# Strassen products and output units of a second feed-forward layer: the order in which they are issued

## The chip, the cores and the metric

One core of a Trainium2 chip runs the whole program. The metric is the device time of one execution in microseconds; the kernel before takes 963.16 us in the median of three runs (962.7 to 963.23).

## The reference

Linear attention over 4 batches of 8 heads (576 positions, 64 dimensions, 128 random features in two signs), and behind it two feed-forward layers on the 2304 tokens of 512 channels. Only the second layer bears on the change:

```python
def _moe2_ref(x, w_in, w_out):
    h = x @ w_in              # 2304x512 by 512x2048
    r = np.maximum(h, 0.0)
    g = r * r
    return (g @ w_out).astype(np.float32)   # 2304x2048 by 2048x512
```

## The kernel before, in words

Every fp32 matrix product is made of three matmuls on fp32r values: an operand is split into a high part (a rounded copy, ScalarE) and a low part (the difference, VectorE), and high x high, high x low and low x high are added up in PSUM.

The program has three stages: attention, the first layer (`feed_forward`, blocks of 512 tokens: `G1`, the elementwise part, `G2`), and the second layer. Within a stage the order is written out by hand: each engine runs its instructions in the order of the program text, and waits by semaphores where data or a buffer isn't ready.

The second layer works on 3 groups of 768 tokens. For a group, 8 *pairs* of 128-column chunks of the hidden dimension are computed, so 24 pairs s = 0 to 23 in all. The four quarters 11, 12, 21 and 22 of a pair's hidden block (two chunks by two halves of 384 tokens) come from **seven products** in Strassen's way instead of eight (`product`, L598, its matmuls at L611). A product is 6 matmuls of 128x128 weights by 384 columns. The products write two PSUM banks in turn: 0, 2, 4, 6 the one and 1, 3, 5 the other; with the next pair the two change places. Between the products `quarters` (L616) takes the partial sums out and combines them:

- after product 0, 2 and 4 ScalarE copies the bank (s1, s2, s3: L628, L637, L642); products 2, 4 and 6 add to that bank, so they must wait for these copies;
- after product 1 VectorE adds s1 and the other bank to quarter 11 (L634), after product 3 it makes a part of 12 (L640), which L644 lessens by s3, and after product 5 it makes 21 (L647);
- after product 6 VectorE finishes 12 (L652) and ScalarE makes 22 by a Relu (L655), then a square (L656).

`square` (L625, VectorE) applies relu and square to 11, 21 and 12. `hi_lo` (L590) splits a finished quarter: high part at L592 on ScalarE, low part at L593 on VectorE.

The **output units** (`unit`, L658, matmuls at L666) multiply the quarters of the pair before by the output weights: 12 units for each pair, unit n of three matmuls of 512 columns, that adds into one of six other PSUM banks. Units 0 to 5 use quarters 11 and 21 in turn, units 6 to 11 use 12 and 22. In the last pair of a group every second unit is followed by the eviction of its bank (L676 on ScalarE or L678 on VectorE) and a store.

`second_step(s, k)` (L701) issues product k of pair s, its `quarters`, `UNITS_AT[k]` units of pair s - 1, the pieces of operand preparation that fall there (`refill`, L682: subtractions L445 and splits L451 and L452 at pairs 7, 8, 15 and 16), and the DMA that reads back a piece of weights for pair s + 2 (`read_back`, L695, issued on SP at L493). `second_layer` (L715) calls it for s = 1 to 24 and k = 0 to 6, and after each step `convert_late`. Pair 0's products are issued earlier, among the last `G2` of the first layer (`FIRST_AT`, L728), followed by the evictions of the first layer's last block (L402, L404).

`convert_late(now)` (L577) issues what is due before `now + 1` of the preparation of 16 tiles of output weights, which come in 64-bit form. A tile with the time `at` of `LATE_AT` is loaded by SP (L472) at `at - 2`; at `at` its *words* are taken apart (L238, L240, both ScalarE); at `at + 2` they are *joined* (L259, L261, L268 on VectorE, then L263 on POOL); at `at + 4` the tile is *split* (L281 on ScalarE, L285 on VectorE). The clock of these times counts 7 for a pair:

```python
LATE_AT = (-1, 1, 3, *range(5, 44, 3))
LATE_STAGE = 2

def convert_late(now):
    while late_events and late_events[0][0] < now + 1:
        late_events.pop(0)[1]()
```

So tiles 3 to 15 have the times 5, 8, 11, ... 41, and the last split is due at 45, in pair 6.

Of the kernel before, what the change touches and what calls it, by code (L numbers as in the profile page):

```python
# [12 lines left out]
ACTF = mybir.ActivationFunctionType  # L13
# [13 lines left out]
    ("A11", "B11", 0, True), ("A12", "B21", 1, True), ("S2", "T2", 0, False), ("S4", "B22", 1, True),  # L27
    ("S3", "T3", 0, False), ("A22", "T4", 1, True), ("S1", "T1", 0, False),
)
UNITS_AT = (2, 2, 2, 2, 2, 1, 1)  # L30
AHEAD_TILES = tuple(("in", n) for n in range(16))
AHEAD_FIRST, AHEAD_NEXT, AHEAD_STAGE, AHEAD_LOAD = 14.0, 8.6, 7.0, 9.5
LATE_AT = (-1, 1, 3, *range(5, 44, 3))
# [130 lines left out]
def attention_ffn_kernel(  # L164
# [11 lines left out]
    nc = tc.nc  # L176
# [12 lines left out]
    def f(t):  # L189
        return t.bitcast(F32)  # L190

    with tc.manual_schedule():
# [15 lines left out]
        def bank(tag, shape=(P, 512), name=None):  # L208
            return ps.tile(list(shape), F32, tag=tag, name=name or tag, bufs=BUFS[tag])
# [225 lines left out]
        NG, NP = NT // GROUP, KFF // 2  # L435
        raw_x, wc, spill, h2_t, g2_t, b2 = {}, {}, {}, {}, {}, {}
# [140 lines left out]
# [3 lines that stand above are left out]
# [10 lines left out]
        def hi_lo(s, name):  # L590
            g, t = quarter(s, name), h2_t.pop((s, name))
            nc.scalar.activation(out=g[:, 0], in_=t, func=ACTF.Copy)  # L592
            nc.vector.tensor_tensor(out=g[:, 1], in0=t, in1=f(g[:, 0]), op=ALU.subtract)  # L593
# [4 lines left out]
        def product(s, k):  # L598
            if k == 0 and s == 0:
                b2["m"] = [bank("pj", name="m") for _ in range(2)]  # L600
            p = s % NP
            wn, xn, to, start = PRODUCTS[k]
            i = next(i for i in range(4) if wn in PIECES[i])
            o = 2 * P * PIECES[i].index(wn)
            wh, wl = (w_piece(s, i, hl)[:, o:o + 2 * P] for hl in range(2))
            xh, xl = x_parts(xn)
            m = banks(s)[to]
            for q in range(2):
                sl = slice(q * P, (q + 1) * P)
                for n, (l, r) in enumerate(((wh, xh), (wh, xl), (wl, xh))):  # L610
                    nc.tensor.matmul(  # L611
                        out=m, lhsT=l[:, sl], rhs=r[:, q], start=start and q == 0 and n == 0, stop=q == 1 and n == 2,
                        skip_group_check=True,
                    )

        def quarters(s, k):  # L616

            a, b = banks(s)

            def new(name, tag="pq"):  # L620
                t = h2_t[s, name] = work(tag, [P, HALF], F32, "t")
                return t

            def square(t):
                nc.vector.scalar_tensor_tensor(out=t, in0=t, scalar=0.0, in1=t, op0=ALU.max, op1=ALU.mult)  # L625

            if k == 0:
                nc.scalar.activation(out=new("s1", "kq"), in_=a, func=ACTF.Copy)  # L628
                if s > 0:
                    hi_lo(s - 1, "12")  # L630
                    hi_lo(s - 1, "22")
            elif k == 1:
                t = new("11")
                nc.vector.tensor_tensor(out=t, in0=b, in1=h2_t.pop((s, "s1")), op=ALU.add)  # L634
                square(t)
            elif k == 2:
                nc.scalar.activation(out=new("s2", "kq"), in_=a, func=ACTF.Copy)  # L637
                hi_lo(s, "11")
            elif k == 3:
                nc.vector.tensor_tensor(out=new("12"), in0=b, in1=h2_t.pop((s, "s2")), op=ALU.add)  # L640
            elif k == 4:
                nc.scalar.activation(out=new("s3", "pk"), in_=a, func=ACTF.Copy)  # L642
                t = h2_t[s, "12"]
                nc.vector.tensor_tensor(out=t, in0=t, in1=h2_t[s, "s3"], op=ALU.subtract)  # L644
            elif k == 5:
                t = new("21")
                nc.vector.tensor_tensor(out=t, in0=h2_t.pop((s, "s3")), in1=b, op=ALU.subtract)  # L647
                square(t)
            else:
                hi_lo(s, "21")  # L650
                t = h2_t[s, "12"]
                nc.vector.tensor_tensor(out=t, in0=a, in1=t, op=ALU.add)  # L652
                square(t)
                t = new("22")
                nc.scalar.activation(out=t, in_=a, func=ACTF.Relu)  # L655
                nc.scalar.activation(out=t, in_=t, func=ACTF.Square)  # L656

        def unit(s, n):  # L658
            m, f_ = divmod(n, 2)
# [39 lines left out]
                    read_piece(s + 2, i)  # L699

        def second_step(s, k):  # L701
            if s < NG * NP:
                product(s, k)
                quarters(s, k)
            elif k == 0:
                for name in ("12", "22"):
                    hi_lo(s - 1, name)
            if s > 0:
                n0 = sum(UNITS_AT[:k])
                for n in range(n0, n0 + UNITS_AT[k]):  # L710
                    unit(s - 1, n)
            refill(s, k)
            read_back(s, k)

        def second_layer():  # L715
            for s in range(1, NG * NP + 1):
                for k in range(7):
                    second_step(s, k)
                    convert_late(7 * s + k)

        def share(j, i):
            if j == 0 and i >= START_0:
# [67 lines left out]
        with ExitStack() as actx:  # L790
# [172 lines left out]
            run, steps = {}, {}  # L963
# [164 lines left out]
```

## Time and profile before

| | |
|---|---|
| Median of three runs | 963.16 us (962.7 to 963.23) |
| The profiled execution's own time | 963.75 us |
| Its span, first to last instruction | 962.0 us |
| TensorE busy | 953.5 us (99%) |
| VectorE busy | 657.4 us (68%) |
| ScalarE busy | 536.9 us (56%) |
| GpSimd busy | 169.0 us (18%) |
| TensorE's granted clock over the span | 0.999 of full speed |
| Second layer: from pair 0's first product to the last matmul | 574.6 to 957.9 us |

The span is the profiled execution's; what lies between it and the execution's time is outside of the trace. In the trace PE is TensorE, PEld its weight loads, DVE VectorE, ACT ScalarE, POOL GpSimd, SP the engine that issues nearly all DMAs (SPq its queue). A matmul's end is modelled, so the distance of starts is the measure of TensorE's rhythm. In the timeline neighbours of one line are merged (x6 is six instructions), and brackets give the engine's idle time before an instruction and what ended it.

### The profile page before, as it was taken

Reading aid. Unit: us, or ns where it says so; the run is one execution under the profiler, and the core shown is the slowest. Engines: PE = TensorE matmul, PEld = TensorE weight load, DVE = VectorE, ACT = ScalarE, POOL = GpSimd, SP = SyncE. Lnnn points to the kernel's source line nnn. Section 1 sums busy time; section 2 is a strip of 40 time slices with the busy share of each in tenths; the row PEclk is TensorE's granted clock in tenths of the full one; section 3 lists DMA queues with packets and bytes.
Section 4 is the critical chain, followed back from the end, with each engine's and each line's share of the span. In section 5 each row is a group of like instructions: output and inputs, shape, how many; then the busy total and the mean of one; then the engine's idle time right before and its main releaser. Section 6 shows DMA issues by size and latency. Waiting matters only on the chain.

```text
span 962.0 us, 15555 instructions
## 1 busy us (share of the span) xinstructions
PE 953.5 (99%) x5865; PEld 824.9 (86%) x5865; DVE 657.4 (68%) x1137; ACT 536.9 (56%) x1053; POOL 169.0 (18%) x146
## 2 busy tenths in 40 slices
PE   8999999999999999999999999999999999999998
PEld 7878888788899888888888888989889898989897
DVE  6787887589967777867867667777663444744344
ACT  4988886667766656666655654555352323423223
POOL 1666765100002033213200011221000000000000
PEclk9999999999999999999999999999999999999999
DMA  7566633152021155334335206656563435544411
GB/s 245 174 204 229 189 121 101 32 204 79 1 89 41 29 190 168 120 131 155 132 132 149 71 22 208 199 184 190 172 194 112 121 113 184 164 138 126 118 36 65
DMA packets 52282, 128.26 MB, mean 133 GB/s; under 512 B 6384, under 2 KB 12144, under 8 KB 52208
## 3 DMA queue, kind: packets, MB, share of 16 engines
q1 hardware_dynamic: 52064, 127.21, 41.2%
q8 instruction: 46, 0.75, 0.3%
q14 instruction: 28, 0.23, 0.1%
q10 hardware_dynamic: 144, 0.07, 0.0%
HBM read 102.99 MB, written 24.19 MB: 132 GB/s over the span
## 4 chain that ended last, share of the span: by engine, by line
PE 94%; DMA 2%; ACT 2%; DVE 1%; POOL 0%; SPq 0%; issue 0%; DVEq 0%; ACTq 0%; POOLq 0%
PE acc L385 21%; PE acc L666 20%; PE m L611 18%; PE h L314 7%; PE h L315 7%; PE h L316 7%; PE kv L867 5%; PE nm L913 3%; PE pj L833 2%; PE nm L921 2%; PE tp L890 1%; PE kv L875 1%; PE pj L842 1%; DMA raw<-in_dram 1%; ACT eq L901 1%; ACT e L859 0%
## 5 line engine op out<-in xcount | busy, mean ns | idle before, releaser
L666 PE MATMUL acc<-w,g 128*128 128x512 f32 x864 | 226.0, 394 | 0.0
L385 PE MATMUL acc<-g,w 128*128 128x512 f32 (+1 forms) x960 | 208.6, 368 | 0.0
L385 PEld LDWEIGHTS acc<-g,w 128*128 128x128 f32 x960 | 168.0, 189 | 30.5 <-DVE g L345 0.6
L666 PEld LDWEIGHTS acc<-w,g 128*128 128x128 f32 x864 | 159.7, 188 | 23.3
L611 PE MATMUL m<-xc,wc 128*128 128x384 f32 x864 | 173.7, 336 | 0.8 <-DVE t L634 0.8
L611 PEld LDWEIGHTS m<-xc,wc 128*128 128x128 f32 x864 | 154.5, 188 | 14.2 <-DVE t L634 1.3
L314 PE MATMUL h<-xs,w 128*128 128x512 f32 (+1 forms) x320 | 117.9, 369 | 0.0
L315 PE MATMUL h<-xs,w 128*128 128x512 f32 (+1 forms) x320 | 117.7, 368 | 0.0
L316 PE MATMUL h<-xs,w 128*128 128x512 f32 (+1 forms) x320 | 117.7, 368 | 0.0
L593 DVE TENSOR_TENSOR g<-t,g 128x384 fp32r<-128x384 f32 x96 | 53.6, 579 | 77.5 <-ACT g L592 77.4
L342 ACT ACTIVATE g<-tr 128x512 fp32r<-128x512 f32 (+1 forms) x80 | 47.0, 589 | 69.2 <-PE acc L385 46.7
L263 POOL TENSOR_TENSOR mag<-mag,raw 128x512 int32<-128x512 int32 x36 | 48.1, 1337 | 213.1 <-ACT tr L335 92.1
L592 ACT ACTIVATE g<-t 128x384 fp32r<-128x384 f32 x96 | 47.3, 518 | 64.8 <-DVE t L625 64.5
L337 DVE SCALAR_TENSOR_TENSOR tr<-tr,h 128x512 f32<-128x512 f32 (+1 forms) x80 | 50.5, 631 | 35.5 <-ACT tr L335 35.2
L345 DVE TENSOR_TENSOR g<-tr,g 128x512 fp32r<-128x512 f32 (+1 forms) x80 | 52.8, 660 | 24.7 <-ACT g L342 24.7
L314 PEld LDWEIGHTS h<-xs,w 128*128 128x128 f32 x320 | 60.3, 189 | 10.2 <-issue 0.2
L316 PEld LDWEIGHTS h<-xs,w 128*128 128x128 f32 x320 | 60.3, 188 | 10.1
L315 PEld LDWEIGHTS h<-xs,w 128*128 128x128 f32 x320 | 60.4, 189 | 9.9
L848 DVE TENSOR_REDUCE m<-pj 128x4 f32<-128x512 f32 (+1 forms) x80 | 49.9, 624 | 19.3 <-PE pj L833 11.7
L867 PEld LDWEIGHTS kv<-v,e 128*128 128x128 f32 x512 | 60.1, 192 | 3.4 <-issue 1.8
L867 PE MATMUL kv<-v,e 128*128 128x65 f32 x512 | 62.1, 274 | 0.7 <-ACT e L859 0.6
L330 DVE SCALAR_TENSOR_TENSOR tr<-tr,h 128x512 f32<-128x512 int32 (+1 forms) x80 | 50.2, 628 | 16.0 <-ACT tr L328 15.5
(92 smaller groups left out, 1339.8 us busy)
## 6 DMA issues: line engine op xcount, KB each, us to landing
wc<-sp SPq DMA_DIRECT2D x72, 512.0 KB
raw<-in_dram SPq DMA_DIRECT2D x48, 512.0 KB
xbuf<-in_dram SPq DMA_DIRECT2D x16, 512.0 KB
sp<-xbuf SPq DMA_DIRECT2D x15, 512.0 KB
kq<-in_dram SPq DMA_DIRECT2D x16, 384.0 KB
wc<-sp SPq DMA_DIRECT2D x24, 256.0 KB
v<-in_dram SPq DMA_DIRECT2D x16, 330.0 KB
dn<-db SPq DMA_DIRECT2D x32, 144.0 KB
```

What stands on the lines that cost most here:

```text
L314: nc.tensor.matmul(out=hps, lhsT=ih[:, kk, :], rhs=xh, start=kk == 0, stop=False)
L315: nc.tensor.matmul(out=hps, lhsT=ih[:, kk, :], rhs=xl, start=False, stop=False)
L316: nc.tensor.matmul(out=hps, lhsT=il[:, kk, :], rhs=xh, start=False, stop=kk == KDM - 1)
L330: nc.vector.scalar_tensor_tensor(out=r, in0=t.bitcast(I32), scalar=-C1, in1=h_t[c], op0=ALU.mult, op1=ALU.add)
L337: nc.vector.scalar_tensor_tensor(out=t, in0=r, scalar=1.0, in1=h_t.pop(c), op0=ALU.subtract, op1=ALU.mult, reverse0=True)
L345: nc.vector.tensor_tensor(out=g[:, 1], in0=t, in1=f(g[:, 0]), op=ALU.subtract)
L385: nc.tensor.matmul(out=acc[m][:, 0:n], lhsT=l, rhs=r, start=c == 0 and i == 0, stop=c == KFF - 1 and i == 2)
L593: nc.vector.tensor_tensor(out=g[:, 1], in0=t, in1=f(g[:, 0]), op=ALU.subtract)
L611: nc.tensor.matmul(out=m, lhsT=l[:, sl], rhs=r[:, q], start=start and q == 0 and n == 0, stop=q == 1 and n == 2, skip_group_check=True,)
L666: nc.tensor.matmul(out=acc[m], lhsT=g[:, l, sl], rhs=w[:, r], start=p == 0 and f_ == 0 and i == 0, stop=p == NP - 1 and f_ == 1 and i == 2,)
L848: nc.vector.tensor_reduce(out=m[:, 0:n], in_=pj[:, 0:n, :], axis=AX.X, op=ALU.max, apply_absolute_value=True)
L867: nc.tensor.matmul(out=acc[:, s, h, 0:D + 1], lhsT=e[:, t, s, :], rhs=v_t[u][:, t, h, 0:D + 1], start=t == 0 and h == 0 and s == 0, stop=F ...
```

## The change

The table `UNITS_AT` (2, 2, 2, 2, 2, 1, 1 units behind the seven products) goes. In its place a pair's products are issued in three runs, products 0 and 1, products 2 and 3, and products 4, 5 and 6, with four units of the pair before behind each run. `convert_late` is called after each unit instead of after each step, with a `now` that grows by 7/12 from unit to unit, starting from 7s.

The square of 11 moves from behind product 1 to behind product 2, and its split from product 2 to product 3. The squares of 21, 12 and 22 and the splits of 21, 12 and 22 are put into a list `owed` when product 6 is issued, and one entry is taken from it after each unit: four behind the last run of the pair, two behind the first two units of the next. Before pair 1 two entries are taken at once. In the last step, that has units alone, `refill` and `read_back` are no longer called.

```diff
--- before.py
+++ after.py
@@ -27,7 +27,7 @@
     ("A11", "B11", 0, True), ("A12", "B21", 1, True), ("S2", "T2", 0, False), ("S4", "B22", 1, True),
     ("S3", "T3", 0, False), ("A22", "T4", 1, True), ("S1", "T1", 0, False),
 )
-UNITS_AT = (2, 2, 2, 2, 2, 1, 1)
+SHORT_RUNS = (((0, 1), 4), ((2, 3), 4), ((4, 5, 6), 4))
 AHEAD_TILES = tuple(("in", n) for n in range(16))
 AHEAD_FIRST, AHEAD_NEXT, AHEAD_STAGE, AHEAD_LOAD = 14.0, 8.6, 7.0, 9.5
 LATE_AT = (-1, 1, 3, *range(5, 44, 3))
@@ -613,6 +613,8 @@
                         skip_group_check=True,
                     )
 
+        owed = []
+
         def quarters(s, k):
 
             a, b = banks(s)
@@ -626,18 +628,15 @@
 
             if k == 0:
                 nc.scalar.activation(out=new("s1", "kq"), in_=a, func=ACTF.Copy)
-                if s > 0:
-                    hi_lo(s - 1, "12")
-                    hi_lo(s - 1, "22")
             elif k == 1:
                 t = new("11")
                 nc.vector.tensor_tensor(out=t, in0=b, in1=h2_t.pop((s, "s1")), op=ALU.add)
-                square(t)
             elif k == 2:
                 nc.scalar.activation(out=new("s2", "kq"), in_=a, func=ACTF.Copy)
-                hi_lo(s, "11")
+                square(h2_t[s, "11"])
             elif k == 3:
                 nc.vector.tensor_tensor(out=new("12"), in0=b, in1=h2_t.pop((s, "s2")), op=ALU.add)
+                hi_lo(s, "11")
             elif k == 4:
                 nc.scalar.activation(out=new("s3", "pk"), in_=a, func=ACTF.Copy)
                 t = h2_t[s, "12"]
@@ -645,15 +644,16 @@
             elif k == 5:
                 t = new("21")
                 nc.vector.tensor_tensor(out=t, in0=h2_t.pop((s, "s3")), in1=b, op=ALU.subtract)
-                square(t)
             else:
-                hi_lo(s, "21")
                 t = h2_t[s, "12"]
                 nc.vector.tensor_tensor(out=t, in0=a, in1=t, op=ALU.add)
-                square(t)
                 t = new("22")
                 nc.scalar.activation(out=t, in_=a, func=ACTF.Relu)
-                nc.scalar.activation(out=t, in_=t, func=ACTF.Square)
+                owed.extend((
+                    lambda: square(h2_t[s, "21"]), lambda: hi_lo(s, "21"), lambda: square(h2_t[s, "12"]),
+                    lambda: nc.scalar.activation(out=t, in_=t, func=ACTF.Square),
+                    lambda: hi_lo(s, "12"), lambda: hi_lo(s, "22"),
+                ))
 
         def unit(s, n):
             m, f_ = divmod(n, 2)
@@ -699,24 +699,28 @@
                     read_piece(s + 2, i)
 
         def second_step(s, k):
-            if s < NG * NP:
-                product(s, k)
-                quarters(s, k)
-            elif k == 0:
-                for name in ("12", "22"):
-                    hi_lo(s - 1, name)
-            if s > 0:
-                n0 = sum(UNITS_AT[:k])
-                for n in range(n0, n0 + UNITS_AT[k]):
-                    unit(s - 1, n)
+            product(s, k)
+            quarters(s, k)
             refill(s, k)
             read_back(s, k)
 
         def second_layer():
-            for s in range(1, NG * NP + 1):
-                for k in range(7):
-                    second_step(s, k)
-                    convert_late(7 * s + k)
+            steps = NG * NP
+            for _ in range(2):
+                owed.pop(0)()
+            for s in range(1, steps + 1):
+                n, now = 0, 7.0 * s
+                for ks, units in SHORT_RUNS:
+                    if s < steps:
+                        for k in ks:
+                            second_step(s, k)
+                    for _ in range(units):
+                        unit(s - 1, n)
+                        n += 1
+                        if owed:
+                            owed.pop(0)()
+                        convert_late(now)
+                        now += 7 / 12
 
         def share(j, i):
             if j == 0 and i >= START_0:
```

## Rows read from the trace of the kernel before

**Rows 1.** The page, engines and groups (busy us, mean ns, idle us)
```profile
PE 953.5 (99%) x5865; PEld 824.9 (86%) x5865; DVE 657.4 (68%) x1137; ACT 536.9 (56%) x1053; POOL 169.0 (18%) x146
...
L611 PE MATMUL m<-xc,wc 128*128 128x384 f32 x864 | 173.7, 336 | 0.8 <-DVE t L634 0.8
...
L593 DVE TENSOR_TENSOR g<-t,g 128x384 fp32r<-128x384 f32 x96 | 53.6, 579 | 77.5 <-ACT g L592 77.4
```

**Rows 2.** Timeline, product 0 of pairs 4 and 5 (start us, us, engine, line)
```profile
635.85 1.22 PE L611 MATMUL m<-xb,wc 128*128 128x384 f32 x6
...
651.54 1.22 PE L611 MATMUL m<-xb,wc 128*128 128x384 f32 x6
```

**Rows 3.** Timeline from pair 1's product 0 to pair 2's
```profile
587.47 1.20 PE L611 MATMUL m<-xb,wc 128*128 128x384 f32 x6
...
589.48 0.49 ACT L655 ACTIVATE t<-m 128x384 f32<-128x384 f32 x1 [1.09 <-DVE t L652]
...
589.96 1.28 DVE L404 COPY ot<-acc 128x512 f32<-128x512 f32 x2
...
590.03 1.31 PE L611 MATMUL m<-xc,wc 128*128 128x384 f32 x6
...
604.48 1.22 PE L611 MATMUL m<-xb,wc 128*128 128x384 f32 x6
```

**Rows 4.** Timeline, pair 0's products among the first layer's last matmuls
```profile
574.59 1.23 PE L611 MATMUL m<-xb,wc 128*128 128x384 f32 x6
...
576.69 2.92 PE L385 MATMUL acc<-g,w 128*128 128x512 f32 x12
...
579.45 3.31 PE L611 MATMUL m<-xc,wc 128*128 128x384 f32 x18
...
580.72 0.49 ACT L637 ACTIVATE t<-m 128x384 f32<-128x384 f32 x1 [3.36 <-PE m L611]
...
582.60 2.92 PE L385 MATMUL acc<-g,w 128*128 128x512 f32 x12
```

**Rows 5.** Timeline, pair 7 from product 4 to its Relu
```profile
692.66 1.21 PE L611 MATMUL m<-xc,wc 128*128 128x384 f32 x6
...
693.90 0.49 ACT L642 ACTIVATE t<-m 128x384 f32<-128x384 f32 x1 [3.23 <-PE m L611]
...
697.03 0.55 DVE L647 TENSOR_TENSOR t<-t,m 128x384 f32<-128x384 f32 x1
...
698.09 0.95 DVE L452 TENSOR_TENSOR xc<-xr,xc 128x768 fp32r<-128x768 f32 x1
...
700.07 0.49 ACT L655 ACTIVATE t<-m 128x384 f32<-128x384 f32 x1 [1.34 <-DVE t L652]
```

**Rows 6.** Timeline, pair 4, a join's first instruction and the splits behind it
```profile
646.52 0.42 DVE L259 TENSOR_SCALAR mag<-mag 128x512 f32<-128x512 f32 x1
...
649.79 0.63 ACT L281 ACTIVATE w<-mag 128x512 fp32r<-128x512 f32 x1 [1.34 <-POOL mag L263]
...
650.46 0.69 DVE L285 TENSOR_TENSOR w<-mag,w 128x512 fp32r<-128x512 f32 x1
```

**Rows 7.** Timeline, pair 3, product 3, a load and its words
```profile
627.48 1.21 PE L611 MATMUL m<-xc,wc 128*128 128x384 f32 x6
...
629.46 0.33 SPq L472 DMA_DIRECT2D raw<-in_dram  x1
...
634.03 0.67 ACT L238 ACTIVATE mag<-raw 128x512 f32<-128x512 f32 x1 [2.39 <-DMA raw<-in_dram]
```

**Rows 8.** Two stretches at the end: busy us by engine, clock, DMA
```profile
957.00:958.00 1.00, 0.93 (x5) 0.42 (x3) 1.00 (x2) 0.00 (x0) 0.00 (x0) 1.00 0.90 336
...
960.00:962.00 2.00, 0.00 (x0) 0.00 (x0) 0.00 (x0) 0.00 (x0) 0.00 (x0) 0.54 0.21 77
```

**Rows 9.** Timeline, TensorE's first two groups of matmuls
```profile
1.58 2.50 PE L820 MATMUL nm<-eq 128*128 128x512 f32 x5 [1.58 <-DVE eq L814]
...
4.01 3.79 PE L833 MATMUL pj<-wph,kq 64*128 64x128 f32 x32
```

## The prediction

> **What bounds the kernel now.** I read the page first: TensorE is busy 953.5 us of a span of 962.0, and at the products it idles 0.8 us in all, behind VectorE's L634 [rows 1]. So TensorE's own rhythm and its stalls set the time; another engine counts only where it makes TensorE wait. Then I read the timeline of the second layer step by step. A step, from one pair's product 0 to the next pair's, takes 635.85 to 651.54 = 15.69 us for pair 4 [rows 2], and the other 21 of pairs 2 to 23 are like it. Pair 1's is longer, 587.47 to 604.48 = 17.01 us [rows 3]: there the 0.8 us lies. So two things can be won in the second layer: the cost of switching between products and units, and the 1.3 us of pair 1. Whatever else the change moves can only make a new wait.
>
> **Longer runs.** The trace has runs of the new lengths, where pair 0's products lie among the first layer's last matmuls, which have the shape of a unit's. Twelve matmuls of products take 574.59 to 576.69 = 2.10 us, twelve of unit shape 2.76, eighteen of products 579.45 to 582.60 = 3.15 [rows 4]. The new step is 2 x 2.10 + 3.15 + 3 x 2.76 = 15.63 against 15.69. Rounding leaves 0.04 to 0.06; I take 0.05 x 22 = **-1.1 us**.
>
> **Which distance shrinks.** A product's sum is read by ScalarE or VectorE before the product after next may write that bank. The reader starts 1.24 us after the product's first matmul (692.66 to 693.90) and takes 0.49 [rows 5]. Nearly all these distances are now two products and four units, 4.9 us, and were no longer before. One shrinks: from product 4 to product 6, by way of ScalarE's copy s3 (L642). Before, three units and product 5 lay between; now product 5 alone does, so product 6 is due 2.10 us after product 4's start, and the copy ends at 1.73 if ScalarE is free. The pattern stands in the trace once: products 2, 3 and 4 of pair 0 are one run, the copy L637 ends at 580.72 + 0.49 = 581.21, product 4 is due at 579.45 + 2.10 = 581.55, and the run shows no wait [rows 4]. A free ScalarE thus costs nothing; one that is late by more than 0.34 us stalls TensorE. What stands ahead of s3 in ScalarE's queue decides.
>
> **What is put ahead of it.** The late weights are converted by due times: words (ScalarE), join (VectorE, then POOL), split (ScalarE's high half waits for POOL). What is due at 7s + 5 was issued after step 5, so behind s3; now it is issued behind the eighth unit, just ahead of product 4 and s3. By LATE_AT that is a split in pairs 1 and 4, words in pair 3, a join (no ScalarE) in 2 and 5, nothing from 6 on.
>
> *Pair 4.* The join is due behind the fifth unit, after product 3's L640 and the low half of 11. Counting from the start of product 3's last matmul: L640 0.37 to 0.92, the low half (0.58 [rows 1]) to 1.5, the join from 1.55, and ScalarE's split 3.27 later (646.52 to 649.79 [rows 6]), 4.82. s3 starts 0.55 behind it and ends at 5.86. Product 6 was due at 0.17 + 2.76 + 1.07 + 1.04 = 5.04. From a release to the matmul it is 0.06 (L655 ends 589.97, the matmul starts 590.03), and a run that begins from a stall takes 0.1 more [rows 3]: **+1.0 us**. Before, this very split waited 1.34 us for POOL [rows 6] with nothing urgent behind it. Behind s3 stand VectorE's L644 and L647 and the Relu; four units come before those are wanted, so the stall is paid once.
>
> *Pair 3.* Its words wait for a load that SP can issue only behind the read-back that waits for product 3. Product 3's last matmul started at 627.48 + 0.87 = 628.35, the load was issued at 629.46, and the words began at 634.03, after ScalarE had waited 2.39 us for the DMA [rows 7]: 5.68 behind that last matmul. Two words and then s3, each about 0.58 behind the one before, put s3's end at 7.3 against 5.04: **+2.4 us**. The wait was there before; what covered it was s3's place ahead of it, and that is gone.
>
> *Pair 1.* VectorE enters it with the first layer's last evictions (1.28 us [rows 3]), and the squares and splits that now stand behind the units queue behind those. From product 6 of pair 0 (586.43) on: L652 587.67 to 588.2, evictions to 589.5, square 21 to 590.1, ScalarE's high half to 590.65, low half to 591.25, L634 591.85, square 12 592.4, a low half of weights (0.69 [rows 6]) 593.15, join. Its split starts 3.27 later, 596.45, and ends at 597.1 [rows 6]; low half of weights 597.8, low half of 22 598.35, square 11 598.95, L640 599.5, low half of 11 600.1, next join; its split at 603.4, s3 to 604.45. Product 6 starts at 604.5, the next pair at 604.5 + 1.07 + 0.1 + 2.76 = 608.4 against 604.48 [rows 3]: **+3.9 us**, the old wait included. TensorE's earlier stalls in this step hide behind the chain.
>
> *Pairs 7 and 15* fill the next group's operands. Behind product 4 VectorE has L644, two fill steps, L647 (697.03), the low half L452 (698.09, so 5.43 after product 4's start, 0.95 long), then L652 (0.55), and 0.1 later ScalarE's Relu L655, which waits for L652 [rows 5]. The Relu ends 7.55 after product 4's start; the next pair's product 1 is due at 2.10 + 1.04 + 2.76 + 1.07 = 6.97. With release and restart 0.7 each: **+1.4 us**. Before, six units lay in that distance; now four.
>
> **The clock.** In pair 1 TensorE would idle from 601.1 to 604.5. At the trace's end it falls idle near 957.9, and the granted clock of 960 to 962 averages 0.54 [rows 8], so it went to 1.2 GHz after some 2.2 us without a matmul. What a fall costs is bounded by the start of the trace: five matmuls of 512 columns take 2.50 us, twice the later rate, and 32 small ones until 7.80 are slow too [rows 9]; 6.2 us at half rate lose 3.1. Between 0 and 3.1 I take the middle, **+1.5 us**, once, as only pair 1's gap is clearly longer than that of the end. The Trainium skill (TensorE: Matmul & The Clock Gate, "HAM oscillation — how this bites in real kernels") warns that idle gaps between bursts of matmuls let the clock be gated down again. The end of this trace agrees; by that rule alone, with a fall in pair 1 and one in pair 3, the term would be twice as large.
>
> **Elsewhere nothing.** The moved squares and splits add no instruction; in a usual step 21 is wanted by the next step's second unit, over 4 us later, and 12 and 22 by its seventh and eighth. SP's and POOL's queues keep their order. The last step loses its idle fill steps, for which nobody waits.
>
> **The sum:** -1.1 + 1.0 + 2.4 + 3.9 + 1.4 + 1.5 = +9.1 us. On the profiled execution's own 963.75 (span 962.0) that is 972.9; the median of the runs, 963.16, lies 0.6 lower, so I predict 972.3.
>
> **The rivals.** *The clock stays up*: the same waits without the fall, 970.8. For it: the only fall shown is at the end. Against it: the gap of 3.4 us. Chance 0.25. *A late copy in every step*: something small sits on ScalarE, and s3 misses its 0.34 us by 0.15 in 23 steps, +3.5: 975.8. Against it: ScalarE idles 3.23 us before s3 [rows 5]. Chance 0.08. *Faster*: ScalarE and VectorE run the conversions during the four units and s3 is never late; then 1.1 and 1.3 are won, 960.8. It decides at product 6: s3 done before 2.0 us after product 4's start, in every pair. For it: the clean run of eighteen [rows 4]. Against it: ScalarE's waits of 1.34 and 2.39 us in the very instructions that now precede s3 [rows 6, 7]. Chance 0.07. *About the same*: one conversion alone stalls, and the gains pay for it, 962 to 965. Chance 0.05. The forecast has 0.55.
>
> **How the numbers follow.** A measurement of this kernel tells about 0.2%, 1.9 us, from no change. Forecast, steady clock and late copies lie above that: slower 0.88, same 0.05, faster 0.07. The range goes down to 967.5 (no fall, pair 1 at 1.5, pair 3 at 1.5) and up to 976.5, where a fall at 3.1, a second one, or the late copies lie. It leaves out the faster and the unchanged case and the tails.
>
> **What would show it.** The waits of the changed kernel should name TensorE at L611 behind ScalarE's L642 in pairs 1, 3 and 4 alone, some 3.4, 2.3 and 0.9 us, and behind L655 as pairs 8 and 16 begin, with L281 or L238 right ahead of each late L642. A usual step should take 15.64, and the granted clock should dip once, behind 601. I am wrong if TensorE's idle time in the second layer is under 1.3 us, or if L642 is late in steps without a conversion.

## The result and the profile after

| | before | after |
|---|---|---|
| Median (four runs each) | 962.93 us (962.12 to 963.23) | 971.73 us (971.1 to 972.27) |
| Profiled execution | 963.75 us | 972.19 us |
| Its span | 962.0 us | 970.4 us |
| Granted clock over the span | 0.999 | 0.996 |

The fourth run of the kernel before (962.12 us) moves its median from the 963.16 that the prediction started from to 962.93. The ratio is 1.0091, with a 95% interval of 1.0076 to 1.0106: the kernel became slower by 0.9%.

In the listing after the change the copies s1, s2 and s3 stand at L630, L635 and L641, the additions to 11, 12 and 21 at L633, L638 and L646, L649 ends quarter 12, L651 is the Relu and L627 the square. L611 and L666 are the products' and the units' matmuls as before. First the products' group on the page of the changed kernel (columns as in [rows 1]):

```profile
L611 PE MATMUL m<-xc,wc 128*128 128x384 f32 x864 | 164.2, 337 | 5.9 <-ACT t L641 5.1
```

The products' group was idle for 0.8 us behind VectorE [rows 1]; it is idle for 5.9 now, and 5.1 of it stands behind ScalarE's copy s3. The waits of the changed kernel over the second layer (us in total, times, longest) say how often:

```profile
PE m L611 <- ACT t L641: 5.1, 3, 2.9
...
PE m L611 <- ACT t L651: 0.6, 2, 0.3
```

So there are three waits for s3 and two for the Relu. The timeline gives each its place. In it are product 0 of pairs 1 to 6 and what stood ahead of each late copy and ahead of the late Relu of pair 7:

```profile
586.75 1.21 PE L611 MATMUL m<-xb,wc 128*128 128x384 f32 x6
...
602.13 0.63 ACT L281 ACTIVATE w<-mag 128x512 fp32r<-128x512 f32 x1 [1.66 <-POOL mag L263]
602.67 0.47 ACT L641 ACTIVATE t<-m 128x384 f32<-128x384 f32 x1
...
603.20 1.32 PE L611 MATMUL m<-xc,wc 128*128 128x384 f32 x6 [2.88 <-ACT t L641]
604.36 4.50 PE L666 MATMUL acc<-w,g 128*128 128x512 f32 x12
604.56 0.56 DVE L649 TENSOR_TENSOR t<-m,t 128x384 f32<-128x384 f32 x1
605.03 0.55 DVE L627 SCALAR_TENSOR_TENSOR t<-t 128x384 f32<-128x384 f32 x1
...
608.70 1.23 PE L611 MATMUL m<-xb,wc 128*128 128x384 f32 x6
...
624.34 1.23 PE L611 MATMUL m<-xb,wc 128*128 128x384 f32 x6
...
632.25 0.33 SPq L472 DMA_DIRECT2D raw<-in_dram  x1
...
636.58 0.66 ACT L238 ACTIVATE mag<-raw 128x512 f32<-128x512 f32 x1 [4.54 <-DMA raw<-in_dram]
637.68 0.47 ACT L641 ACTIVATE t<-m 128x384 f32<-128x384 f32 x1
...
638.20 1.81 PE L611 MATMUL m<-xc,wc 128*128 128x384 f32 x6 [1.86 <-ACT t L641]
...
643.69 1.23 PE L611 MATMUL m<-xb,wc 128*128 128x384 f32 x6
...
655.04 0.63 ACT L281 ACTIVATE w<-mag 128x512 fp32r<-128x512 f32 x1 [2.97 <-POOL mag L263]
655.57 0.47 ACT L641 ACTIVATE t<-m 128x384 f32<-128x384 f32 x1
...
656.10 1.32 PE L611 MATMUL m<-xc,wc 128*128 128x384 f32 x6 [0.41 <-ACT t L641]
...
660.02 1.23 PE L611 MATMUL m<-xb,wc 128*128 128x384 f32 x6
...
675.66 1.23 PE L611 MATMUL m<-xb,wc 128*128 128x384 f32 x6
...
706.42 0.96 DVE L452 TENSOR_TENSOR xc<-xr,xc 128x768 fp32r<-128x768 f32 x1 [0.45 <-ACT xc L451]
...
707.94 0.49 ACT L651 ACTIVATE t<-m 128x384 f32<-128x384 f32 x1 [1.55 <-DVE t L649]
...
708.48 1.31 PE L611 MATMUL m<-xc,wc 128*128 128x384 f32 x6 [0.32 <-ACT t L651]
```

In pair 1 the split L281 waits for POOL, s3 waits behind the split, and product 6 behind s3. In pair 3 the words L238 wait for their load, in pair 4 a split waits for POOL again. In pair 7 the Relu is started only after L649, which stands behind the low half L452 on VectorE. The twelve matmuls behind product 6 of pair 1 are recorded with 4.50 us, where the same run took 2.92 among pair 0's products [rows 4]. The windows of the changed kernel (columns as in [rows 8]) say why:

```profile
604.70:608.00 3.30, 3.30 (x10) 2.56 (x9) 2.64 (x6) 2.49 (x5) 0.00 (x0) 0.50 0.50 159
...
638.20:638.70 0.50, 0.50 (x3) 0.50 (x4) 0.50 (x2) 0.00 (x0) 0.00 (x0) 1.00 0.56 213
...
638.80:642.10 3.30, 3.30 (x11) 2.84 (x10) 1.86 (x4) 1.40 (x4) 0.00 (x0) 0.50 0.29 68
```

The granted clock is 0.50, so 1.2 GHz, behind both gaps, and 1.00 before the second fall. The step lengths, as distances from one product 0 to the next in the two timelines, are the account of the change:

| step (pair) | before | after | difference |
|---|---|---|---|
| 1 | 17.01 | 21.95 | +4.94 |
| 3 | 15.69 | 19.35 | +3.66 |
| 4 | 15.69 | 16.33 | +0.65 |
| 8 and 16 | 15.69 each | 16.23 each | +1.08 |
| the other 17 of pairs 2 to 22 | 15.687 each | 15.640 each | -0.80 |
| all | | | **+9.53** |

The span grew by 8.4 (970.4 - 962.0). Of the rest -0.72 lies ahead of pair 0's first product (573.87 against 574.59, [rows 4]); in the ten experiments, which also keep that part's work, it lies between 572.8 and 574.4, so I take it for scatter between executions. Another -0.4 lies behind pair 23's product 0: 28.06 us from there to the end of the span before, 27.69 after. Most of it, 0.3, lies behind the last matmul (4.03 us against 3.73, and 3.7 in every experiment too). In the kernel before the copy of the last bank but one (L678, 957.49) stands on VectorE behind two splits of the last step's idle fill steps (L452, 955.55, 2.02 us together); in the changed kernel the same copy waits for TensorE alone. That these fill steps delayed the last stores is likely, but no run takes them out alone.

### The profile page after: what moved, and what is told of

It reads as the page before. It is cut to its first block, busy times and chain, and to the rows that moved or that the text cites. A ratio compares the mean times of both kernels' runs of the same rounds, so it can differ in the third digit from the quotient of the medians.

```text
span 970.4 us, 15613 instructions
## 1 busy us (share of the span) xinstructions
PE 957.7 (99%) x5865; PEld 827.4 (85%) x5865; DVE 643.5 (66%) x1133; ACT 532.4 (55%) x1050; POOL 169.1 (17%) x146
## 4 chain that ended last, share of the span: by engine, by line
PE 89%; DVE 3%; ACT 3%; DMA 3%; POOL 1%; issue 0%; SPq 0%; ACTq 0%; POOLq 0%; DVEq 0%
PE acc L666 19%; PE acc L385 18%; PE m L611 17%; PE h L314 6%; PE h L315 6%; PE h L316 6%; PE kv L871 6%; PE nm L917 3%; PE pj L837 3%; PE nm L925 2%; DMA raw<-in_dram 2%; PE tp L894 1%; DMA sp<-xbuf 1%; PE kv L879 1%; PE pj L846 1%
## 5 line engine op out<-in xcount | busy, mean ns | idle before, releaser
L666 PE MATMUL acc<-w,g 128*128 128x512 f32 x864 | 213.4, 396 | 0.4 <-DVE g L593 0.2
L666 PEld LDWEIGHTS acc<-w,g 128*128 128x128 f32 x864 | 163.1, 190 | 33.3 <-DVE g L593 1.4
L611 PE MATMUL m<-xc,wc 128*128 128x384 f32 x864 | 164.2, 337 | 5.9 <-ACT t L641 5.1
L611 PEld LDWEIGHTS m<-xc,wc 128*128 128x128 f32 x864 | 152.9, 188 | 11.6 <-ACT t L641 6.1
L593 DVE TENSOR_TENSOR g<-t,g 128x384 fp32r<-128x384 f32 x96 | 51.3, 552 | 16.1 <-ACT g L592 16.0
L334 ACT ACTIVATE tr<-tr 128x512 f32<-128x512 f32 (+1 forms) x80 | 46.5, 581 | 21.5 <-DVE tr L332 21.1
```

The lines of the kernel that those rows point to most:

```text
L611: nc.tensor.matmul(out=m, lhsT=l[:, sl], rhs=r[:, q], start=start and q == 0 and n == 0, stop=q == 1 and n == 2, skip_group_check=True,)
L666: nc.tensor.matmul(out=acc[m], lhsT=g[:, l, sl], rhs=w[:, r], start=p == 0 and f_ == 0 and i == 0, stop=p == NP - 1 and f_ == 1 and i == 2,)
```

## The experiments

All start from the changed kernel. A time without an interval is that of one execution; beside it stands the kernel before on the same chip (one execution too, or the median of 21). The two bounds behind a ratio are its 95% interval. Steps are read from the timelines as above. The theory on trial: the loss is made of separate late entries in ScalarE's queue, one behind each late conversion and one behind the fill steps, and of clock falls that follow the longest gaps. The rival: the new order as such (longer runs, less distance, splits moved behind units) costs.

**One load a unit earlier (pair 3 alone).**

```diff
-                events += stages(("out", n), LATE_AT[n], LATE_STAGE, LATE_STAGE, load, split)
+                events += stages(("out", n), LATE_AT[n], LATE_STAGE, LATE_STAGE + (n == 10), load, split)
```

> Only tile 10's load of late weights is moved, one unit of the due times earlier, so that SP issues it ahead of product 3 of pair 3 instead of behind it. Theory (in pair 3 product 6 waits for s3, s3 for the words ahead of it on ScalarE, and those for this load): the words begin before product 4 ends, product 6 of pair 3 follows product 5 after 1.04 us, TensorE's idle 1.86 us there goes and with it the second fall of the clock; step 3 takes 15.64 instead of 19.35, the total falls by 3.7 to about 968. Pairs 1 and 4 stay as they are (21.95 and 16.33). Rival (the two words themselves, or the fuller VectorE, make s3 late, not the load): step 3 stays above 16.5 and the total within 1 us of 971.7.

It took 967.57 us (before: 963.89). Step 3 fell from 19.35 to 15.64; steps 4, 8 and 16 stayed, step 1 was 22.13. Its timeline in pair 3:

```profile
626.17 0.36 SPq L472 DMA_DIRECT2D raw<-in_dram  x1
...
631.05 0.66 ACT L238 ACTIVATE mag<-raw 128x512 f32<-128x512 f32 x1
...
633.17 3.31 PE L611 MATMUL m<-xc,wc 128*128 128x384 f32 x18
634.43 0.49 ACT L641 ACTIVATE t<-m 128x384 f32<-128x384 f32 x1 [2.15 <-PE m L611]
```

Issued one unit earlier in the program, the load no longer stands behind the read-back that waits for product 3. The words are done before product 4 begins, products 4 to 6 run as eighteen matmuls without a break, and s3 waits for TensorE, not the reverse. The whole of step 3's loss, the clock fall included, hung on one place in SP's queue.

**Two splits a unit later (pairs 1 and 4).** The splits of tiles 4 and 11 alone come one unit later, so behind s3.

```diff
-                yield at + 2 * d, lambda: sends.append(split(t, at))
-                yield at + 2.5 * d, lambda: sends.pop(0)()
+                late = 0.5 if t[1] in (4, 11) else 0.0
+                yield at + (2 + late) * d, lambda: sends.append(split(t, at))
+                yield at + (2.5 + late) * d, lambda: sends.pop(0)()
```

> Only the splits of late tiles 4 and 11 come one unit of the due times later, so that they stand behind product 6 instead of right ahead of s3. Theory (s3 waits behind a split that waits for POOL): in pair 4 the stall goes, step 4 takes 15.64 instead of 16.33. In pair 1 s3 then waits only for the words of tile 5, which ended at 600.5, so product 6 starts near 601 instead of 603.2, the gap is under 1 us, the clock does not fall there, and step 1 takes about 18.2 instead of 21.95. Pair 3 stays at 19.35. Total about 967.3. Rival (VectorE's backlog in pair 1 holds s3 by way of the high half of 11, whatever the split does): step 1 stays above 21.

It took 967.74 us (before: 963.89). Step 4 fell to 15.62, step 1 to 18.30; step 3 stayed at 19.40. Its timeline in pairs 1, 3 and 4 (lines one higher than in the changed kernel), and the window behind pair 3's product 6:

```profile
600.97 1.33 PE L612 MATMUL m<-xc,wc 128*128 128x384 f32 x6 [0.59 <-ACT t L642]
...
634.45 1.48 PE L612 MATMUL m<-xc,wc 128*128 128x384 f32 x6 [1.90 <-ACT t L642]
...
649.65 3.31 PE L612 MATMUL m<-xc,wc 128*128 128x384 f32 x18
```

```profile
635.50:638.00 2.50, 2.50 (x8) 2.02 (x7) 1.44 (x3) 1.38 (x4) 0.00 (x0) 0.50 0.38 80
```

Pair 4's wait was the split alone: its products 4 to 6 are eighteen matmuls without a break. In pair 1 a gap of 0.59 us is left, for s3 there now stands behind the words of tile 5. Pair 3 is as it was, with its fall.

**The fill steps one product earlier (pairs 8 and 16).**

```diff
-                todo = ((), (0,), (3, 4), (1,), (2, 5), (6,), ())[k]
+                todo = ((), (0,), (3, 4), (1, 2, 5), (6,), (), ())[k]
```

> Only the order of the next group's operand preparation in pairs 7 and 15 changes: steps 2 and 5 are issued behind product 3 instead of product 4, step 6 behind product 4 instead of 5. Theory (product 1 of the next pair waits for the Relu, the Relu for L649 behind these on VectorE): steps 8 and 16 take 15.64 instead of 16.23, the total falls by 1.2 to about 970.5. Rival (four units are too short a distance for the Relu in any order): steps 8 and 16 stay at 16.2. A third outcome, a new stall in steps 7 and 15 because L640 or s3 is now late: these steps rise above 15.64.

It took 969.17 us (before: 963.89). Steps 8 and 16 went from 16.23 to 15.64. Its timeline in pair 3 and at the end of pair 7:

```profile
637.92 1.32 PE L611 MATMUL m<-xc,wc 128*128 128x384 f32 x6 [1.99 <-ACT t L641]
...
702.58 0.55 DVE L646 TENSOR_TENSOR t<-t,m 128x384 f32<-128x384 f32 x1
703.05 0.55 DVE L649 TENSOR_TENSOR t<-m,t 128x384 f32<-128x384 f32 x1
...
703.69 0.49 ACT L651 ACTIVATE t<-m 128x384 f32<-128x384 f32 x1 [2.02 <-DVE t L649]
```

L649 follows L646 at once, where the low half L452 stood between them. The Relu is done at 703.69 + 0.49 = 704.18, and product 1 starts at 706.16. This run also showed something not asked for. In pair 3, which the edit doesn't touch, product 6 waited a little longer than in the changed kernel, but the clock did not fall and step 3 took 17.92 in place of 19.35. The gap is the first row above; the window behind it:

```profile
638.00:641.00 3.00, 3.00 (x15) 2.65 (x16) 2.06 (x5) 1.07 (x3) 0.00 (x0) 1.00 0.24 38
```

So the same wait without the fall: 17.92 - 15.64 = 2.28 us, with a gap 0.13 longer than the changed kernel's. Of the changed kernel's 3.71 (19.35 - 15.64) the wait is then 2.28 - 0.13 = 2.15, and the rest, 1.56, is the fall.

**The gap of pair 1 filled with matmuls.** Eleven matmuls whose sum nobody reads stand between products 5 and 6 of pair 1; the waits stay as they are.

```diff
+                            if s == 1 and k == 6:
+                                for _ in range(11):
+                                    nc.tensor.matmul(
+                                        out=acc[4], lhsT=g2_t[0, "11"][:, 0, 0:P], rhs=weights[1, 1, 0][:, 0],
+                                        start=True, stop=True,
+                                    )
```

> Added: 11 matmuls of 512 columns between products 5 and 6 of pair 1, into an accumulator bank that no unit has begun yet; they fill TensorE's gap of 2.9 us and change no result. Theory (the gap let the clock fall, and the fall costs 1.6 us): no granted clock of 1.2 GHz behind pair 1, product 6 still starts near 603.2, step 1 takes 20.4 instead of 21.95, total about 970.1. Rival (the slow matmuls behind the gap come from something else, such as the restart of the weight loads or the transfers running then): the slow matmuls stay and step 1 is not shorter, or longer by the added work. The second fall, behind pair 3, should stay in either case.

It took 970.82 us (before: 963.89). Step 1 went from 21.95 to 20.40. Timeline of pair 1, and the window behind its product 6:

```profile
599.29 2.69 PE L718 MATMUL acc<-w,g 128*128 128x512 f32 x11
...
602.35 1.33 PE L611 MATMUL m<-xc,wc 128*128 128x384 f32 x6 [0.37 <-ACT t L641]
603.53 2.92 PE L666 MATMUL acc<-w,g 128*128 128x512 f32 x12
```

```profile
602.30:606.20 3.90, 3.85 (x18) 3.38 (x19) 3.16 (x7) 1.82 (x6) 0.00 (x0) 1.00 0.36 113
```

The twelve unit matmuls took 2.92 again. A fall costs 21.95 - 20.40 = **1.55 us**; what is left of step 1 is the wait itself. Pair 3's gap was longer in this run (2.88 us idle, step 20.39), and the clock fell behind it as before (0.50 from 638.2 to 641.5).

**Four runs instead of three.** Product 6 gets two units between itself and products 4 and 5, which gives s3 back two of the three units of distance that the change took.

```diff
-SHORT_RUNS = (((0, 1), 4), ((2, 3), 4), ((4, 5, 6), 4))
+SHORT_RUNS = (((0, 1), 4), ((2, 3), 4), ((4, 5), 2), ((6,), 2))
```

> Only the last run is cut: products 4 and 5 with two units behind them, then product 6 with two units; conversions, splits and fill steps keep their places between units. Theory (the stalls come from the distance between product 4 and product 6, which is now 1.38 us longer by two units): in pair 4 the stall goes (step 4 under 15.8 instead of 16.33); in pair 3 and pair 1 TensorE's idle time shrinks by about 1.4, to some 0.5 and 1.5 us, too short for the clock to fall in pair 3; step 3 about 16.4, step 1 about 19. Steps 8 and 16 stay about 0.6 above the others, since the four units between product 4 and the next product 1 are still four. A usual step is within 0.06 of 15.64, as the number of runs is between the two kernels'. Total about 966. Rival (ScalarE's order alone decides, at any distance): the idle times stay as they are and the total is above 970.

It took 966.57 us (before: 963.36). Steps 1, 3 and 4 fell to 19.60, 16.62 and 15.64. The idle time before product 6 is 1.49, 0.69 and none, and the clock stayed at 1.00 in pairs 1 and 3. Timeline of pairs 1 and 3, and the window behind pair 1's product 6:

```profile
603.16 1.33 PE L611 MATMUL m<-xc,wc 128*128 128x384 f32 x6 [1.49 <-ACT t L641]
...
635.87 1.33 PE L611 MATMUL m<-xc,wc 128*128 128x384 f32 x6 [0.69 <-ACT t L641]
```

```profile
603.10:606.00 2.90, 2.84 (x14) 2.58 (x15) 2.83 (x7) 0.01 (x1) 0.00 (x0) 1.00 0.23 21
```

Steps 8 and 16 stayed at 16.23 and 16.25, as expected. Step 2 took 16.09, which was not: its product 1 starts 1.29 us behind product 0 instead of 1.04, right behind a late Relu. The rival (idle times as they were, total above 970) falls. The wait has two conditions, the short distance and the late entry ahead of s3. Taking away either mends pair 4; the distance mends pairs 1 and 3 in part, the moved load pair 3 wholly. A usual step remained 15.64 although it changes between products and units once more.

**The squares and splits back in their old places.** The runs and the calls of `convert_late` stay new; `quarters` is the old one.

```diff
             if k == 0:
...
+                if s > 0:
+                    hi_lo(s - 1, "12")
+                    hi_lo(s - 1, "22")
...
+                square(t)
...
+                hi_lo(s, "11")
...
-                owed.extend((
-                    lambda: square(h2_t[s, "21"]), lambda: hi_lo(s, "21"), lambda: square(h2_t[s, "12"]),
-                    lambda: nc.scalar.activation(out=t, in_=t, func=ACTF.Square),
-                    lambda: hi_lo(s, "12"), lambda: hi_lo(s, "22"),
-                ))
+                nc.scalar.activation(out=t, in_=t, func=ACTF.Square)
```

> The new runs and the calls of the conversions after each unit stay; the squares and splits go back to the products where they stood before the change. Theory (the runs and the conversions' places make the stalls, the moved squares and splits none; they only help the Relu): steps 3 and 4 stay as in the changed kernel (about 19 and 16.3), a usual step 15.64; steps 8 and 16, where VectorE is full, grow from 16.23 to about 17.6, since square 21, its high part and its low part come ahead of L649 again; pair 1's product 1 waits 1.5 us for the Relu instead of 0.4. Total 974 to 976. Rival (the moved squares and splits are part of the loss): steps 1, 8 and 16 get shorter, total under 971.

It took 972.26 us (before: 962.72). Steps 1, 8 and 16 became longer, not shorter: 22.48, 16.75 and 16.77; step 3 took 18.15 and step 4 16.15. In pair 8 product 1 idles 0.84 us for the Relu, where it idled 0.32. Timeline of pair 3 from product 6 on, and of pair 8:

```profile
638.94 1.34 PE L611 MATMUL m<-xc,wc 128*128 128x384 f32 x6 [2.21 <-ACT t L644]
640.12 2.92 PE L668 MATMUL acc<-w,g 128*128 128x512 f32 x12
...
708.01 1.31 PE L611 MATMUL m<-xc,wc 128*128 128x384 f32 x6 [0.84 <-ACT t L657]
```

At pairs 1, 8 and 16 the direction was as expected, the size smaller. Step 3 missed: about 19 was expected, and the wait was longer than in the changed kernel (2.21 us idle), but the clock did not fall behind it, and the twelve unit matmuls took 2.92. That accounts for most of what the total stayed under its 974 to 976. The rival, that the moved squares and splits are part of the loss, falls: with these runs they save about half a microsecond at pairs 1, 8 and 16 each. At pair 4 alone they cost a little, 16.33 - 16.15 = 0.18 us.

**All three edits together**, with the split shift for all late tiles and the load shift from tile 4 on:

```diff
-                yield at + 2 * d, lambda: sends.append(split(t, at))
-                yield at + 2.5 * d, lambda: sends.pop(0)()
+                yield at + 2.5 * d, lambda: sends.append(split(t, at))
+                yield at + 3 * d, lambda: sends.pop(0)()
...
-                events += stages(("out", n), LATE_AT[n], LATE_STAGE, LATE_STAGE, load, split)
+                events += stages(("out", n), LATE_AT[n], LATE_STAGE, LATE_STAGE + (n >= 4), load, split)
...
-                todo = ((), (0,), (3, 4), (1,), (2, 5), (6,), ())[k]
+                todo = ((), (0,), (3, 4), (1, 2, 5), (6,), (), ())[k]
```

> The runs of the changed kernel, with the causes taken away together: loads of late tiles 4 to 15 one unit of the due times earlier, all late splits one unit later, and the next group's preparation earlier in pairs 7 and 15. Theory (the stalls are all the loss, the runs themselves a small gain): steps 2 to 23 take 15.64, step 1 between 16.2 and 17.2 (its Relu and the first units still wait a little), no fall of the clock; total 1 to 2 us under the kernel before, ratio about 0.9985. Rival (something else in the change costs time too, the tail or the moved squares): ratio 1.002 or more though no step from 2 on has a stall.

Median 962.93 us over 11 runs (before: 963.36), ratio 1.0004 [0.9995, 1.0013], where about 0.9985 was expected. In the profiled execution (962.79 us) every step from 2 to 22 is 15.64: there the whole of the loss is gone, and the gain of 0.047 a step stands. Step 1 missed: 18.11, still 1.10 longer than in the kernel before, which takes the gain back. The timeline shows a new wait at its start:

```profile
589.21 1.28 DVE L404 COPY ot<-acc 128x512 f32<-128x512 f32 x2
...
590.99 0.52 ACT L592 ACTIVATE g<-t 128x384 fp32r<-128x384 f32 x1 [1.45 <-DVE t L627]
...
591.56 2.71 PE L666 MATMUL acc<-w,g 128*128 128x512 f32 x9 [1.43 <-ACT g L592]
```

The second unit waits 1.43 us for the high part of 21, whose square stands behind the first layer's evictions on VectorE. Four of the 11 runs took 964.57 to 965.33 us with a mean clock of 0.998, the other seven 962.03 to 963.29 (one of these at 0.998 too). A clock fall in some executions would fit that; only the profiled execution has a timeline, so it is not shown.

**Seven products in one run.** As the last, and in pairs 9 to 14 and 17 to 22 all seven products in one run with twelve units behind them:

```diff
+ONE_RUN = (((0, 1, 2, 3, 4, 5, 6), 12),)
...
-                for ks, units in SHORT_RUNS:
+                for ks, units in ONE_RUN if one_run(s) else SHORT_RUNS:
...
-                        if owed:
-                            owed.pop(0)()
+                        for _ in range(2 if one_run(s + 1) and not one_run(s) else 1):
+                            if owed:
+                                owed.pop(0)()
```

> As the one before, and pairs 9 to 14 and 17 to 22, which have no conversions, fill steps or evictions, issue all seven products in one run and all twelve units of the pair before in another; the owed squares and splits come behind the first six units. Theory (a reader that finds its engine free costs nothing even with one product in between, margin 0.2 to 0.34 us; what a step pays is each change between products and units): a step of these pairs takes about 42 x 0.1733 + 36 x 0.2267 + 0.07 = 15.51, that is 0.13 less, 1.6 us over 12 steps; ratio to the kernel before about 0.997. Rival (the margin is too small: the copies or L633 and L638 come late with only one product in between): stalls at products 3 to 6 in each of these steps, which then take more than 15.64.

Median 963.9 us over 11 runs, ratio 1.0005 [0.9996, 1.0014], where about 0.997 was expected. The steps with one run took 15.52 to 15.57, but steps 9 and 17 took 16.11 and 16.13: there s1 is late behind the group's evictions and product 2 idles 0.30 us. In the profiled execution (962.85 us) gain and loss cancel. The rival, a late copy or addition in each of the twelve steps, falls with the other ten.

**The first two owed entries ahead of the evictions.** As all three edits together, with tiles 0 to 3 keeping their split times, and the square and the split of pair 0's 21 issued before the last block's evictions:

```diff
...
-            for _ in range(2):
-                owed.pop(0)()
...
+                if j == LAST_0:
+                    for _ in range(2):
+                        owed.pop(0)()
                 evict(j)
```

> As e6_all_three, with two differences at pair 1: tiles 0 to 3 keep their old split times, so that no split stands ahead of the first layer's last evictions, and the square and split of pair 0's quarter 21 are issued before those evictions instead of behind them. Theory (in e6 the second unit of pair 1 waited 1.43 us for the high part of 21, which stood behind a split and the evictions): that wait goes, step 1 takes 15.9 to 16.4 instead of 18.11, every later step 15.64, no gap is long enough for the clock to fall; total about 960.9, ratio 0.997 to 0.999. Rival (the evictions' being later now holds the fifth unit's bank, or s1): step 1 stays above 17.

Median 961.97 us over 11 runs (before: 962.96), ratio 0.9989 [0.998, 0.9997]. The second unit's wait is gone, step 1 fell to 17.53 but not as far as expected (15.9 to 16.4). Product 6 still idles 0.52 us in its timeline (lines one higher again), for s3 is behind the words of tile 5, which wait for their load:

```profile
598.21 0.68 ACT L238 ACTIVATE mag<-raw 128x512 f32<-128x512 f32 x1 [0.72 <-DMA raw<-in_dram]
...
599.88 1.33 PE L612 MATMUL m<-xc,wc 128*128 128x384 f32 x6 [0.52 <-ACT t L642]
```

**Both, with one run in ten pairs.** As the last, with one run in pairs 10 to 14 and 18 to 22, away from the evictions:

```diff
...
+        def one_run(s):
+            return s > NP and 1 < s % NP < NP - 1
```

> As e8_owed_first, and pairs 10 to 14 and 18 to 22 issue seven products and twelve units in one run each (pairs 9 and 17, where the evictions of the group before made s1 late, keep the three runs). Theory: each of these ten steps takes 15.52 to 15.57 instead of 15.64, as measured in e7, and none stalls; total 1.0 us under e8. Rival (the first one-run step stalls wherever it stands, since two owed entries are taken per unit ahead of it): steps 10 and 18 take 15.9 or more and the gain is gone.

Median 961.06 us over 11 runs (before: 962.96), ratio 0.9982 [0.9973, 0.9991]: faster than the kernel before by 0.2%, and so than the changed kernel. It is 0.91 us under the run described before, where 1.0 was expected, and steps 10 and 18 took 15.54 and 15.55, so its rival falls. The timeline of a step with one run (products at L613, units at L668), from product 0 to product 0, 15.54 us, and above it products 4 to 6 of pair 1:

```profile
598.11 3.32 PE L613 MATMUL m<-xc,wc 128*128 128x384 f32 x18
...
729.15 1.23 PE L613 MATMUL m<-xb,wc 128*128 128x384 f32 x6
730.21 6.43 PE L613 MATMUL m<-xc,wc 128*128 128x384 f32 x36
...
744.69 1.23 PE L613 MATMUL m<-xb,wc 128*128 128x384 f32 x6
```

Step 1 took 16.73 here and 17.53 in the run described before, with the same program up to there. The difference is the wait of that run: here the words of tile 5 begin at 598.41 without waiting for their load, and products 4 to 6 of pair 1 run as eighteen matmuls without a break. So the length of step 1 hangs on when this one load lands, which the program doesn't fix.

## Why the prediction was right

The predicted 972.3 lies 0.6 us above the measured 971.73, and the forecast case came in: s3 late in pairs 1, 3 and 4, the Relu late in pairs 8 and 16, a clock fall, no late copy in any other step. One of its statements was wrong, the single clock fall, and the closeness of the total is in part luck.

The steps are those of the profiled execution (972.19 us). The terms are compared with the stalls over a step of 15.64, as the prediction counted them, and pair 1's with the 17.01 of the kernel before.

*Longer runs*: -1.1 predicted, -0.05 a step. Measured -0.047 a step, -1.0 over pairs 2 to 22. Right.

*Pair 1*: 3.9 for the waits and 1.5 for the clock, 5.4 in all; measured 4.94, of which 1.55 is the clock and 3.39 the waits. The gap was to be 3.4 us and is 2.88.

*Pair 4*: +1.0, measured 16.33 - 15.64 = 0.69. The mechanism was right; the chain was summed too long, here as in pair 1. The prediction let each VectorE instruction follow its forerunner after the recorded 0.55 and a little; L649 and L627, at 604.56 and 605.03 in the changed kernel's timeline, start 0.47 apart. In pair 4 the join's first instruction to the split also took less, 651.87 to 655.04 = 3.17, not 3.27.

*Pair 3*: +2.4, measured 19.35 - 15.64 = 3.71, and here the prediction was wrong: a fall "once, as only pair 1's gap is clearly longer than that of the end". The wait was sized well: 2.28 in the run in which the clock stayed up, 2.15 here. But the clock fell behind this gap too, for 1.56. The step that failed is taking the one fall at the end of the trace for a bound on the gap that brings one. The prediction had named two falls beside its sum, and two falls of 1.55 and 1.56 came. It had drawn them from the Trainium skill's warning of gaps (TensorE: Matmul & The Clock Gate, "HAM oscillation — how this bites in real kernels"), and read it too widely: that warning is of gaps longer than either of these, 2.88 and 1.86 us, so by the Trainium skill as it stands neither of the two was due.

*Pairs 7 and 15*: 0.7 each; measured 16.23 - 15.64 = 0.59. Right in place and cause; moving the fill steps took all of it away.

*The clock*: 1.5 from the middle of 0 and 3.1, measured 1.55 and 1.56 by two different runs. Its size was right, though the middle of so wide a bound hit it by luck; its count was not.

*Elsewhere nothing*: right in that the moved squares and splits add no wait in a usual step. The run with them put back shows that they help at pairs 1, 8 and 16 and cost 0.18 us at pair 4. That nobody waits for the last step's idle fill steps is probably wrong by the 0.3 us behind the last matmul.

So the sum, +9.5 in the steps against +9.1, came closer than its terms: the second fall (+1.56) was missed, and the waits were taken too long by 0.5 (pair 1), 0.3 (pair 3), 0.3 (pair 4) and 0.2 (pairs 7 and 15). That these nearly cancel is luck.

The rival *clock stays up* falls with the windows at 0.50. *A late copy in every step* falls with the usual step of 15.64 and only three waits. *Faster* was the right reading of the runs and the wrong one of ScalarE's queue: with the conversions, the fill steps and two owed entries moved, 961.97 was measured where that rival gave 960.8.

## What to carry to other kernels

When instructions are regrouped into longer runs, look for the one distance that shrinks, and then for everything that now stands ahead of its reader in that engine's queue: an old wait on a DMA or on another engine, harmless behind the reader, becomes a stall ahead of it. The repair is then not to undo the regrouping but to move the waiting entry by one place. A gap of two microseconds in a stream of matmuls should be priced with and without a clock fall.

## What was not expected of the hardware

**The length of a gap alone does not decide the clock.** It fell behind gaps of 2.88 and 1.86 us (the changed kernel) and 1.90 (two splits later, pair 3), but not behind 2.21 (squares and splits back, pair 3), 1.99 (fill steps earlier, pair 3) or 1.49 (four runs, pair 1). At the end of the trace, from which the prediction took its bound, it fell 2.2 us behind the last matmul in the kernel before; in the run with the load earlier it still stood at 1.00 from 962.10 to 965.70, 3.6 us without a matmul. In the changed kernel product 6 of pair 3 started at full clock (1.00 up to 638.70), and the fall to 0.50 came with TensorE busy again. Among the four runs of the changed kernel the mean clock was 0.996 in two (972.19 and 972.27 us) and 0.998 in two (971.26 and 971.1); 0.998 is what the runs with a single fall have, so the second fall probably comes in some executions and not in others. This is not shown: the two pairs of runs lie 1.05 us apart, less than the 1.56 of a fall, and only the first run has a timeline. The Trainium skill (TensorE: Matmul & The Clock Gate, "What's actually happening") says that the gate's observation runs on its own, not started by the program; that would fit, and no run here tests it. The Trainium skill's warning of gaps, in the section named above, is written for longer ones than these; the traces decide that gaps of 2.88, 1.90 and 1.86 us sufficed.

**A change of shape has no single price.** Seven changes from products to units a step (before) give 15.69 us, three or four 15.64, one 15.52 to 15.57. Three against four made no difference. What sets these prices is not shown.
